# A's scores of a Nyström attention in 32x32 array tiles, transposed to tokens on VectorE

## The chip, the cores and the metric

One NeuronCore of a Trainium2 chip runs the whole kernel. The metric is the device time of one execution in microseconds. Before the change three runs took 265.65, 267.60 and 267.34 us (median 267.34). Engines are named by their profile letters where a view is quoted: PE is TensorE, PEld its weight loads, DVE is VectorE, ACT ScalarE, POOL GpSimd, SP SyncE.

## The reference

The inputs are q, k, v of 8 batches, 8 heads, 576 tokens and 64 dimensions, and two weight matrices of 512x2048 and 2048x512. Each batch goes through a Nyström attention with 32 landmarks, the means of 18 tokens each:

```
q_lm = q.reshape(B, H, 32, 18, D).mean(axis=3)
k_lm = k.reshape(B, H, 32, 18, D).mean(axis=3)
A  = softmax(scale * q @ k_lm^T)       # 576 x 32
Bm = softmax(scale * q_lm @ k_lm^T)    # 32 x 32
C  = softmax(scale * q_lm @ k^T)       # 32 x 576
Z  = Bm^T / (norm_1(Bm) * norm_inf(Bm) + 1e-6)
six times: Z = 2 Z - Z @ Bm @ Z
attention = A @ Z @ C @ v
```

The heads are put side by side as x (4608 tokens, 512 wide), and the result is `silu(x @ w_in) @ w_out`.

## The kernel before

**Stages.** The product Z C v of a batch is folded into w_in, which gives M (tile mb, 256 x 2048 per batch: 8 heads times 32 landmarks on two sets of 128 partitions). So the first layer is hps = M^T A^T, with A transposed (tile AT: landmark and head on the partition, tokens along the row). ScalarE's Silu turns hps into gT, and the second layer, ops, multiplies gT with w_out. ScalarE copies ops out and SyncE stores it.

**The order of work** is written out by hand. The loop at line 877 goes over the batches b; inside it 16 slots s. Each slot issues a piece of the first layer (`l1`, four matmuls), its Silu (`act`), and a counted number of second-layer matmuls (`l2_mm(cnt[s])`, from the lists CNT and REST), and between them lie the attention steps of the next batch, in the object `a` of class Att. With d = 0 from b = 2 on: slots 0 and 1 hold A's scores, B's and C's scores; slot 2 the exponentials (between two loads of ScalarE's function table, Exp and back to Silu); slots 3 to 9 the Newton steps of Z (`ns_mm` on TensorE, `ns_step` on VectorE), with the sums, reciprocals and products that normalise A in slots 4 to 7; slots 9 and 10 the last products of Z and C v (`x_out`, `z_mm`, `z_out`); slots 11 and 13 the M pairs (`m_pair`: mp and mpp). Slots 9, 10, 12 and 14 transpose q and k of the batch after the next on VectorE (`transpose_qk`, qkT), slots 4 and 8 form its landmarks on GpSimd, slot 13 transposes these (`lm_t`, lmc) and slot 15 starts its A scores, if that batch is 4 or later (`early`).

**A's scores before.** From batch 3 on (`sub`), tokens lie on the partition: for each chunk of 128 tokens and each half of the heads, qkT is the stationary operand and bd the moving one. bd is lmc spread block-diagonally over four heads, written by four GpSimd copies per batch (`bd_expand`). Five chunks go in three groups (`a_scores(0)`, `(1)`, `(2)`: 8, 8 and 4 matmuls) through the one-bank buffer "a". After each group VectorE takes the maximum over the 32 landmarks (`a_max`, nm) and subtracts it into xs in SBUF (`a_sub`). One ScalarE instruction takes all exponentials (`a_exp_all`, ex). VectorE sums them (`a_sum`), takes reciprocals (`a_rec`), GpSimd multiplies (`a_mul`, an), and for each chunk SyncE issues a DMA transpose of an into AT.

**Buffers around it.** The pool "h" has two buffers of two banks each. hps, scp (C's scores) and mpp take them in turn: a new user waits until the last reader of the buffer's earlier content is done. Engines execute their instructions in the order of issue.

Of the kernel before, what the change touches and what calls it, by code (L numbers as in the profile page):

```python
# [10 lines left out]
AF = mybir.ActivationFunctionType  # L11
OP = mybir.AluOpType
AX = mybir.AxisListType

# [24 lines left out]
def kernel(  # L41
# [9 lines left out]
    nc = tc.nc  # L51
# [28 lines left out]
    def ps2(nm):  # L80
        return psh.tile([128, 2, 512], FP, tag="h", name=nm)
# [159 lines left out]
    class Att:  # L241
# [300 lines left out]


        def a_first(self):
            self.nm = attp.tile([128, len(TCH), 8], BF, tag="nm", name="nm")
            if self.sub:
                self.xs = attp.tile([128, len(TCH), 256], FP, tag="xs", name="xs", bufs=1)

        def a_start(self):
            if not self.sub:  # L550
                self.a_first()
            self.ex = attp.tile([128, len(TCH), 256], BF, tag="ex", name="ex")
            self.arec = attp.tile([128, len(TCH), 8], FP, tag="arec", name="arec")
            self.an = attp.tile([128, len(TCH), 256], BF, tag="an", name="an")
            self.AT = AT_t[self.b] = attp.tile([128, 2, S], BF, tag="AT", name="AT")

        def a_dims(self, i):
            cc = list(range(2 * i, min(2 * i + 2, len(TCH))))
            return cc[0], len(cc), 128 if self.sub else TCH[cc[0]][1] - TCH[cc[0]][0]


        def a_scores(self, i):
            if i == 0 or self.sub:
                s = psa1("sa")
            elif self.b == 0:
                s = pso1("sa")
            else:
                s = pso1("sa") if i == 1 else self.bb[:, 128:384]
            self.sa[i] = s
            first = True  # L570
            for c in range(2 * i, min(2 * i + 2, len(TCH))):
                c0, c1 = TCH[c]
                if self.sub:
                    c0 = c1 - 128
                o = 256 * (c - 2 * i)
                ov = s[0:c1 - c0, o:o + 256].rearrange("p (r g n) -> p g r n", r=2, g=2)
                for g in range(2):
                    for e in range(2):
                        mm(ov[:, g].rearrange("p r (j l) -> p r j l", l=L),
                           self.qkT[:, 2 * g, c0:c1, e],  # L580
                           self.bd[:, g, :, e].rearrange("p (j r l) -> p r j l", r=2, l=L),
                           start=first, stop=(e == 1))
                        first = False

        def a_max(self, i, eng=nc.vector):
            c, n, pr = self.a_dims(i)
            with nc.allow_low_precision(reason="any shift common to a row's terms is exact"):
                eng.tensor_reduce(  # L588
                    out=self.nm[0:pr, c:c + n, :],
                    in_=self.sa[i][0:pr, 0:256 * n].rearrange("p (c h l) -> p c h l", h=8, l=L),  # L590
                    op=OP.max, axis=AX.X, negate=True)

# [4 lines left out]
                   .to_broadcast((pr, 8 * n, L)), start=False, stop=True)  # L597

        def a_sub(self, i):
            c, n, pr = self.a_dims(i)  # L600
            nc.vector.tensor_tensor(  # L601
                out=self.xs[:, c:c + n, :].rearrange("p c (h l) -> p (c h) l", l=L),
                in0=self.sa[i][:, 0:256 * n].rearrange("p (m l) -> p m l", l=L),
                in1=self.nm[:, c:c + n, :].rearrange("p c h -> p (c h)").unsqueeze(2)
                    .to_broadcast((128, 8 * n, L)), op=OP.add)


        def a_exp_all(self):
# [7 lines left out]
                                 scale=sc if self.mean else sc / SEG)  # L616

        def a_part(self, i):
            c, n, pr = self.a_dims(i)
            return (self.ex[0:pr, c:c + n, :].rearrange("p c (h l) -> p (c h) l", l=L),  # L620
                    self.arec[0:pr, c:c + n, :].rearrange("p c h -> p (c h)"))
# [13 lines left out]
                in1=r.unsqueeze(2).to_broadcast((128, 8, L)), op=OP.mult)  # L635

        def a_rec(self, i, n=1):
            c, _, pr = self.a_dims(i)
            r = self.arec[0:pr, c:min(c + 2 * n, len(TCH)), :].rearrange("p c h -> p (c h)")
            nc.vector.reciprocal(out=r, in_=r)  # L640
# [4 lines left out]
            self.a_mul(i)  # L645

        def a_mul(self, i):
            c, n, pr = self.a_dims(i)
            x, r = self.a_part(i)
            nc.gpsimd.tensor_tensor(  # L650
                out=self.an[0:pr, c:c + n, :].rearrange("p c (h l) -> p (c h) l", l=L), in0=x,
                in1=r.unsqueeze(2).to_broadcast((pr, 8 * n, L)), op=OP.mult)
            if self.by_dma:
                for m in range(c, c + n):
                    c0, c1 = TCH[m]
                    nc.sync.dma_start(out=self.AT[:, :, c0:c1],
                                      in_=self.an[pr - (c1 - c0):pr, m, :], transpose=True)


        def a_transpose(self, k, bank=None):  # L660
# [98 lines left out]
    def l2_mm(n):  # L759

        st = l2_state
        while n > 0 and st["queue"]:
# [18 lines left out]

    CNT = {0: [0, 0, 0, 0, 4, 4, 2, 2, 4, 4, 2, 2, 2, 2, 2, 2],
           1: [2, 2, 2, 2, 2, 6, 8, 8] + [4, 3] * 4,
           2: [5, 4, 12, 14, 3, 3, 3, 2, 4, 3, 3, 3, 4, 3, 3, 3]}
    REST = [5, 4, 12, 12, 3, 3, 2, 2, 4, 4, 4, 3, 4, 3, 4, 3]


# [89 lines left out]
    for b in range(B):  # L877
# [14 lines left out]
        for s in range(NDC):  # L892
# [46 lines left out]
            elif s == d + 1:  # L939
                l1(s)  # L940
                act(s)
                l2_mm(cnt[s])
                if a.sub and not a.early:
                    a.a_scores(1)
                    a.a_max(1)
                    a.a_sub(1)
                if b == 0:

                    transpose_qk(1, ORD[s])
                    a.lm_t(1)  # L950
                    a.bd_expand(0, 2, nc.gpsimd.tensor_copy)
                    for i in (1, 2):
                        a0.a_scores(i)
                        a0.a_max(i)
                a.b_scores()
                a.c_scores()
                if a.early:
                    a.a_scores(2)
                a.b_max()
                a.c_max(0)  # L960
                table(AF.Exp)
# [5 lines left out]
            elif s == d + 2 and a.sub:  # L967
                a.a_start()
                a.c_max(1)
                if not a.early:  # L970
                    l2_mm(4)
                    a.a_scores(2)
                a.a_max(2)
                a.a_sub(2)
                a.c_exp(0)
                a.c_exp(1)
                a.a_exp_all()
                a.b_norm()
                l2_mm(cnt[s] if a.early else cnt[s] - 4)
                table(AF.Silu)  # L980
                l1(s)
            elif s == d + 2:
# [82 lines left out]
            elif s == d + 3:  # L1065
                l1(s)
                act(s - 1)
                act(s)
                l2_mm(2)
                a.f_mm()  # L1070
                a.b_scale()
                a.f_out()


                nc.gpsimd.tensor_copy(out=gate, in_=a.fx[:, :, 0])  # L1075
                l2_mm(cnt[s] - 2)
                a.ns_mm()
            elif s <= d + 8:
                l1(s)
                if s == d + 6:  # L1080
                    a.w_mm()
                a.ns_step()
                act(s)
                if s == d + 4:
                    a.a_sum(0)
                elif s == d + 5:
                    a.a_sum(1)
                elif s == d + 6:
                    a.w_scale()
                    a.w_out()  # L1090
                    a.a_rec(0, 2)
                    a.a_mul(0)
                    a.a_mul(1)
                elif s == d + 7:
                    a.a_norm(2)
                l2_mm(cnt[s])
                a.ns_mm(last=(s == d + 8))
            elif s == d + 9:
                l1(s)
                a.x_out()  # L1100
                act(s)
                l2_mm(cnt[s])
            elif s == d + 10:
                l1(s)
                a.z_mm()
                a.z_out()
                act(s)
                l2_mm(cnt[s])
            else:
                l1(s)  # L1110
                act(s)
                if s in (d + 11, d + 13):
                    a.m_pair(s - d - 11)
                l2_mm(cnt[s])
# [8 lines left out]
            elif b + 2 < B:  # L1123
# [7 lines left out]
                if s == 13 and b > 1:  # L1131
                    ready = Att(b + 2)
                    ready.lm_t(0, 2)
                    ready.bd_expand(0, 2, nc.gpsimd.tensor_copy)
                ts = (9, 10, 12, 14) if d == 0 else (10, 11, 12, 13)
                if s in ts:
                    transpose_qk(b + 2, ORD[ts.index(s)])
                if s == 15 and b == 1:
                    ready = Att(b + 2)
                    ready.lm_t(0, 2)  # L1140
                    ready.bd_expand(0, 2, nc.gpsimd.tensor_copy)
                if s == 15 and ready.early:
                    ready.a_first()
                    ready.a_scores(0)
                    ready.a_max(0)
                    ready.a_sub(0)
            if (b, s) == (0, 3):
                l2_state["queue"] += [(0, 0)]
            elif s == 7:
# [32 lines left out]
```

## Time and profile before

| | |
|---|---|
| median of three runs | 267.34 us (265.65 to 267.60) |
| the profiled execution | 265.63 us, of it the span 263.9 us |
| granted TensorE clock over the span | 1.000 |
| second layer, ops | 576 matmuls, 146.1 us busy |
| first layer, hps | 512 matmuls, 82.8 us busy |
| A's scores, sa from bd and qkT | 152 matmuls, 12.3 us busy |
| Silu, gT from hps | 128 instructions, 82.7 us busy, 651 ns each |
| q/k transposes, qkT | 32 instructions, 38.7 us busy |
| GpSimd's normalising, an | 23 instructions, 20.1 us busy |
| DMA transposes of an into AT | 30 issues, 3.8 us median to landing |

The span runs from the first to the last instruction. The busy share says how long an engine had an instruction in flight. The chain of waits is followed back from the last instruction: at each step to what released it, or to the instruction in front of it on its engine; its pieces in order of time give the start, the time on the chain, the engine, and the tile written. Rows of the groups give line, engine, operation, output and inputs with their sizes, how often, the sum of busy us, the mean ns of one, and the idle time before them with its releaser. A timeline row gives start, duration, engine, line and operation. All matmuls share line 77, since a helper issues them, so they are told apart by their tiles.

### The profile page before, as it was taken

What the parts mean: (1) busy time and instruction counts of PE and PEld (TensorE: products, weight loads), DVE (VectorE), ACT (ScalarE), POOL (GpSimd) and SP (SyncE); (2) the same over time, 40 slices, a digit from 0 to 9 for tenths busy, and PEclk for the clock granted to TensorE, in tenths of its full rate; (3) what the DMA queues carried; (4) which work ended last, traced back from release to release, by engine and by line L of the source; (5) the groups of instructions that cost most, each with busy time, mean ns of one, the idle gap of its engine ahead of it and who ended that gap; (6) DMA issues with size and microseconds to landing.
All of it is one profiled execution on the core that took longest, in us unless ns stands there. A gap on an engine that the chain in (4) does not pass through costs nothing.

```text
span 263.9 us, 6736 instructions
## 1 busy us (share of the span) xinstructions
PE 254.5 (96%) x2755; PEld 143.4 (54%) x2755; DVE 161.1 (61%) x397; ACT 173.1 (66%) x314; POOL 118.3 (45%) x169
## 2 busy tenths in 40 slices
PE   8989989999999999999999999999999999999994
PEld 3647544475555456555655565555555564555541
DVE  5878874558597868876786778686778653000000
ACT  2377955769757785869575966687577947536511
POOL 7716424314698169744885189408950030100000
PEclk9999999999999999999999999999999999999999
DMA  7999999984983962878197927513471612121122
GB/s 222 202 211 206 203 206 219 186 151 75 197 151 78 197 150 41 147 142 182 50 134 164 200 73 98 117 32 112 54 164 40 103 60 67 40 80 42 40 80 80
DMA packets 37790, 32.93 MB, mean 125 GB/s; under 512 B 18816, under 2 KB 29056, under 8 KB 37760
## 3 DMA queue, kind: packets, MB, share of 16 engines
q0 software_dynamic: 14816, 17.76, 41.8%
q1 hardware_dynamic: 22944, 14.75, 22.0%
q8 instruction: 21, 0.34, 0.5%
q14 instruction: 9, 0.07, 0.1%
HBM read 36.70 MB, written 9.44 MB: 175 GB/s over the span
## 4 chain that ended last, share of the span: by engine, by line
PE 85%; DVE 7%; ACT 4%; DMA 2%; issue 1%; POOL 1%; ACTq 0%; POOLq 0%
PE ops L77 46%; PE hps L77 23%; PE lmp L77 3%; PE bb L77 3%; PE sa L77 3%; PE mp L77 2%; DVE cmx L445 2%; DMA raw<-in_k_dram 2%; PE scp L77 1%; PE wp L77 1%; PE mpp L77 1%; ACT eC L455 1%; ACT ex L614 1%; DVE nm L588 1%; PE atp L672 1%
## 5 line engine op out<-in xcount | busy, mean ns | idle before, releaser
L77 PE MATMUL ops<-w_out_sb,gT 128*128 128x512 bf16 x576 | 146.1, 379 | 0.0
L751 ACT ACTIVATE gT<-hps 128x576 bf16<-128x576 f32 (+2 forms) x128 | 82.7, 651 | 55.9 <-PE hps L77 55.2
L77 PE MATMUL hps<-AT,mb 128*128 128x288 bf16 (+2 forms) x512 | 82.8, 286 | 0.4 <-ACT AT L679 0.2
L77 PEld LDWEIGHTS <-gT 128*128 128x128 bf16 x576 | 53.0, 98 | 47.3 <-issue 5.9
L77 PEld LDWEIGHTS <-mb 128*128 128x128 bf16 x512 | 47.7, 98 | 24.9 <-issue 1.8
L200 DVE STREAM_TRANSPOSE qkT<-nat 128x576 f32<-128x576 f32 x32 | 38.7, 1239 | 0.3
L777 ACT COPY ost<-ops 128x512 f32<-128x512 f32 x36 | 21.0, 582 | 12.4 <-PE ops L77 12.3
L650 POOL TENSOR_TENSOR an<-ex,arec 128x512 bf16<-128x512 bf16 (+2 forms) x23 | 20.1, 897 | 18.0 <-DVE arec L640 16.0
L404 DVE SCALAR_TENSOR_TENSOR fx<-fx,bb 128x320 bf16<-128x320 bf16 (+1 forms) x39 | 16.6, 427 | 16.7 <-PE bb L77 16.2
L226 POOL TENSOR_TENSOR lma<-nat 128x1152 f32<-128x1152 bf16 x10 | 23.8, 2376 | 0.0
L717 DVE CAST mb<-mp 128x512 bf16<-128x512 f32 x28 | 18.0, 685 | 9.0 <-PE mp L77 8.9
L1075 POOL CAST gate<-fx 128x2 f32<-128x2 bf16 x6 | 1.1, 186 | 45.5 <-DVE fx L374 45.5
L162 ACT ACT_TABLE_LOAD x16 | 20.5, 1283 | 1.1 <-PEq L1166 0.8
L588 DVE TENSOR_REDUCE nm<-sa 128x16 bf16<-128x512 f32 (+2 forms) x22 | 13.2, 613 | 9.7 <-PE sa L77 9.7
L276 POOL COPY bd<-lmc 32x128 bf16<-32x128 bf16 x32 | 9.2, 286 | 15.0 <-DVE lmc L268 9.0
L77 PEld LDWEIGHTS <-fx 32*32 32x32 bf16 (+1 forms) x168 | 8.1, 93 | 12.6 <-DVE fx L404 3.5
L718 ACT CAST mb<-mpp 128x1024 bf16<-128x1024 f32 x14 | 14.2, 1011 | 0.6 <-PE mpp L77 0.6
L77 PE MATMUL bb<-fx 32*32 32x64 bf16 (+2 forms) x168 | 13.1, 205 | 0.7 <-DVE fx L404 0.3
L77 PEld LDWEIGHTS <-qkT 128*128 128x128 bf16 (+1 forms) x160 | 10.0, 98 | 6.4 <-DVE xs L601 2.7
L625 DVE TENSOR_REDUCE arec<-ex 128x16 f32<-128x512 bf16 (+2 forms) x23 | 13.4, 584 | 0.0
L77 PE MATMUL sa<-bd,qkT 128*128 128x128 bf16 (+1 forms) x152 | 12.3, 221 | 0.2 <-DVE xs L601 0.2
L445 DVE TENSOR_REDUCE cmx<-scp 128x1 f32<-128x576 f32 x16 | 11.9, 752 | 0.8 <-PE scp L77 0.5
(118 smaller groups left out, 259.2 us busy)
## 6 DMA issues: line engine op xcount, KB each, us to landing
out_dram<-ost SPq DMA_DIRECT2D x36, 256.0 KB, 2.2
v<-in_v_dram POOLq DMA_DIRECT2D x8, 576.0 KB, 7.1
nat<-in_k_dram POOLq DMA_DIRECT2D x15, 288.0 KB, 6.0
nat<-in_q_dram POOLq DMA_DIRECT2D x15, 288.0 KB, 7.0
w_in_sb<-in_moe_w_in_dram POOLq DMA_DIRECT2D x4, 512.0 KB, 14.5
w_out_sb<-in_moe_w_out_dram POOLq DMA_DIRECT2D x4, 512.0 KB, 13.5
raw<-in_k_dram SPq DMA_DIRECT2D x1, 576.0 KB, 4.1
raw<-in_q_dram SPq DMA_DIRECT2D x1, 576.0 KB, 5.0
```

The source lines that it names most:

```text
L77: nc.tensor.matmul(out=o, lhsT=lhsT, rhs=rhs, start=start, stop=stop, skip_group_check=True)
L162: nc.scalar.activation(out=spare[:, 1:2], in_=spare[:, 0:1], func=func)
L200: nc.vector.transpose(out=o.rearrange("p (l t) -> p t l", t=SEG), in_=nat_t[b][:, j, :].bitcast(FP).rearrange("p (t l) -> p t l", l=L))
L226: nc.gpsimd.tensor_tensor(out=a1, in0=nat[:, :, 0:3 * w], in1=nat[:, :, 3 * w:6 * w], op=OP.add)
L404: nc.vector.scalar_tensor_tensor(out=n, in0=self.fx, scalar=2.0, in1=self.p, op0=OP.mult, op1=OP.add if self.tiled else OP.subtract)
L445: nc.vector.tensor_reduce(out=mx, in_=self.s[g][:, :, 0:HF], op=OP.max, axis=AX.XY, negate=True)
L588: eng.tensor_reduce(out=self.nm[0:pr, c:c + n, :], in_=self.sa[i][0:pr, 0:256 * n].rearrange("p (c h l) -> p c h l", h=8, l=L), op=OP.max, ...
L650: nc.gpsimd.tensor_tensor(out=self.an[0:pr, c:c + n, :].rearrange("p c (h l) -> p (c h) l", l=L), in0=x, in1=r.unsqueeze(2).to_broadcast(( ...
L717: nc.vector.tensor_copy(out=o[:, r, 0:512], in_=m[r])
L718: nc.scalar.copy(out=o[:, :, 512:1024], in_=m2)
L751: nc.scalar.activation(out=gT_t[b][:, 2 * s:2 * s + 2, o + c0:o + c1], in_=h[:, :, 0:c1 - c0], func=AF.Silu)
L777: nc.scalar.copy(out=ost, in_=st["ps"])
```

## The change

From batch 3 on the landmarks of k become the stationary operand (32x32 slices of lmc) and q's transposed tokens the moving one, in array tiles of 32x32. Scores come in two groups of 288 tokens, 16 matmuls each, landmark on the partition, in a buffer of the pool "h". VectorE transposes them in blocks of 32x32 from PSUM into xs, which puts the token on the partition, and takes the maximum there; GpSimd subtracts it in place. Exponentials, sums, reciprocals and products work on the new layout, two parts for three. The five DMA transposes become two block transposes on VectorE (`a_back`), in slots 9 and 14. `bd_expand` goes for these batches. The q/k transposes of loops 2 to 5 move from slots 9, 10, 12, 14 to 7, 8, 10, 12. Batch 3's second scores move in front of part of the second-layer matmuls of slot 1, and the list CNT for b = 2 is rewritten with the same sum of 72.

```diff
+                self.nm = attp.tile([128, 2, 2, SEG // 2], FP, tag="nmt", name="nm")
...
+        def a_view(self, x):
+            return (x.rearrange("p c n -> p (c n)")[:, 0:2 * S]
+                    .rearrange("p (f r t l) -> p f r t l", f=2, r=2, l=L))
...
         def a_scores(self, i):
-            if i == 0 or self.sub:
+            if self.sub:
+                s = self.sa[i] = ps2("sa")
+                for e in range(2):
+                    for g in range(2):
+                        for h in range(4):
+                            p, j = slice(32 * h, 32 * h + 32), 2 * g + h // 2
+                            mm(s[32 * j:32 * j + 32, h % 2, 0:HF], self.lmc[p, 2 * g + 1, :, e],
+                               self.qkT[p, 2 * g, HF * i:HF * i + HF, e],
+                               start=(e == 0), stop=(e == 1))
+                return
...
         def a_max(self, i, eng=nc.vector):
+            if self.sub:
+                nc.vector.transpose(
+                    out=self.xs[:, i],
+                    in_=self.sa[i][:, :, 0:HF].rearrange("p r (t n) -> p r t n", n=L))
+                eng.tensor_reduce(out=self.nm[:, i], in_=self.xs[:, i], op=OP.max, axis=AX.X,
+                                  negate=True)
+                return
...
         def a_sub(self, i):
-            c, n, pr = self.a_dims(i)
-            nc.vector.tensor_tensor(
-                out=self.xs[:, c:c + n, :].rearrange("p c (h l) -> p (c h) l", l=L),
-                in0=self.sa[i][:, 0:256 * n].rearrange("p (m l) -> p m l", l=L),
-                in1=self.nm[:, c:c + n, :].rearrange("p c h -> p (c h)").unsqueeze(2)
-                    .to_broadcast((128, 8 * n, L)), op=OP.add)
+            nc.gpsimd.tensor_tensor(
+                out=self.xs[:, i], in0=self.xs[:, i],
+                in1=self.nm[:, i].unsqueeze(3).to_broadcast((128, 2, SEG // 2, L)), op=OP.add)
...
         def a_mul(self, i):
+            x, r = self.a_part(i)
+            if self.sub:
+                nc.gpsimd.tensor_tensor(
+                    out=self.an[:, i].rearrange("p r t l -> p (r t) l"), in0=x,
+                    in1=r.unsqueeze(2).to_broadcast((128, SEG, L)), op=OP.mult)
+                return
...
+        def a_back(self, i):
+            nc.vector.transpose(
+                out=self.AT[:, :, HF * i:HF * i + HF].rearrange("p r (t n) -> p r t n", n=L),
+                in_=self.an[:, i])
...
-           2: [5, 4, 12, 14, 3, 3, 3, 2, 4, 3, 3, 3, 4, 3, 3, 3]}
+           2: [5, 8, 12, 12, 3, 3, 2, 2, 4, 3, 3, 3, 3, 3, 3, 3]}
...
             elif s == d + 1:
                 l1(s)
                 act(s)
-                l2_mm(cnt[s])
                 if a.sub and not a.early:
+                    l2_mm(3)
                     a.a_scores(1)
                     a.a_max(1)
                     a.a_sub(1)
+                    l2_mm(cnt[s] - 3)
+                else:
+                    l2_mm(cnt[s])
...
-                if a.early:
-                    a.a_scores(2)
...
             elif s == d + 2 and a.sub:
                 a.a_start()
                 a.c_max(1)
-                if not a.early:
-                    l2_mm(4)
-                    a.a_scores(2)
-                a.a_max(2)
-                a.a_sub(2)
                 a.c_exp(0)
                 a.c_exp(1)
                 a.a_exp_all()
                 a.b_norm()
-                l2_mm(cnt[s] if a.early else cnt[s] - 4)
+                l2_mm(cnt[s])
...
-                elif s == d + 7:
+                elif s == d + 7 and not a.sub:
                     a.a_norm(2)
...
-                    ready.bd_expand(0, 2, nc.gpsimd.tensor_copy)
-                ts = (9, 10, 12, 14) if d == 0 else (10, 11, 12, 13)
+                ts = (7, 8, 10, 12) if d == 0 else (10, 11, 12, 13)
...
+            if nxt and b > 1 and s in (9, 14):
+                a.a_back((9, 14).index(s))
```

More of the change, by code (lines that the diff above doesn't have):

```diff
@@ L544, in a_first @@
         def a_first(self):
-            self.nm = attp.tile([128, len(TCH), 8], BF, tag="nm", name="nm")
             if self.sub:
-                self.xs = attp.tile([128, len(TCH), 256], FP, tag="xs", name="xs", bufs=1)
+                self.nm = attp.tile([128, 2, 2, SEG // 2], FP, tag="nmt", name="nm")
+                self.xs = self.a_view(attp.tile([128, len(TCH), 256], FP, tag="xs", name="xs",
+                                                bufs=1))
+            else:
+                self.nm = attp.tile([128, len(TCH), 8], BF, tag="nm", name="nm")
+        def a_view(self, x):
+            return (x.rearrange("p c n -> p (c n)")[:, 0:2 * S]
+                    .rearrange("p (f r t l) -> p f r t l", f=2, r=2, l=L))
         def a_start(self):
@@ L554, in a_start @@
             self.an = attp.tile([128, len(TCH), 256], BF, tag="an", name="an")
+            if self.sub:
+                self.ex, self.an = self.a_view(self.ex), self.a_view(self.an)
             self.AT = AT_t[self.b] = attp.tile([128, 2, S], BF, tag="AT", name="AT")
@@ L558, in a_dims @@
             cc = list(range(2 * i, min(2 * i + 2, len(TCH))))
-            return cc[0], len(cc), 128 if self.sub else TCH[cc[0]][1] - TCH[cc[0]][0]
+            return cc[0], len(cc), TCH[cc[0]][1] - TCH[cc[0]][0]
         def a_scores(self, i):
-            if i == 0 or self.sub:
+            if self.sub:
[8 more added lines that the diff above has]
+                return
+            if i == 0:
                 s = psa1("sa")
@@ L572, in a_scores @@
                 c0, c1 = TCH[c]
-                if self.sub:
-                    c0 = c1 - 128
                 o = 256 * (c - 2 * i)
@@ L618, in a_part @@
         def a_part(self, i):
+            if self.sub:
+                m = SEG
+                r = self.arec.rearrange("p c h -> p (c h)")[:, m * i:m * i + m]
+                return self.ex[:, i].rearrange("p r t l -> p (r t) l"), r
             c, n, pr = self.a_dims(i)
@@ L637, in a_rec @@
         def a_rec(self, i, n=1):
+            if self.sub:
+                r = self.arec.rearrange("p c h -> p (c h)")[:, 0:2 * SEG]
+                nc.vector.reciprocal(out=r, in_=r)
+                return
             c, _, pr = self.a_dims(i)
@@ L647, in a_mul @@
         def a_mul(self, i):
+            x, r = self.a_part(i)
+            if self.sub:
+                nc.gpsimd.tensor_tensor(
+                    out=self.an[:, i].rearrange("p r t l -> p (r t) l"), in0=x,
+                    in1=r.unsqueeze(2).to_broadcast((128, SEG, L)), op=OP.mult)
+                return
             c, n, pr = self.a_dims(i)
-            x, r = self.a_part(i)
             nc.gpsimd.tensor_tensor(
@@ L946 @@
                     a.a_sub(1)
+                    l2_mm(cnt[s] - 3)
+                else:
+                    l2_mm(cnt[s])
                 if b == 0:
@@ L1140 @@
                     ready.lm_t(0, 2)
-                    ready.bd_expand(0, 2, nc.gpsimd.tensor_copy)
                 if s == 15 and ready.early:
```

## The prediction

> **What bounds the kernel now.** I read the page first: busy shares, then the chain of waits.
>
> ```profile
> PE 254.5 (96%) x2755; PEld 143.4 (54%) x2755; DVE 161.1 (61%) x397; ACT 173.1 (66%) x314; POOL 118.3 (45%) x169
> ...
> PE 85%; DVE 7%; ACT 4%; DMA 2%; issue 1%; POOL 1%; ACTq 0%; POOLq 0%
> ```
>
> TensorE is both the busiest engine and the chain. So I next read the chain in order of time through the head of one batch (the loop over batch 4, whose attention is batch 5's; the heads at 112, 169 and 197 us repeat it, 28.3 us apart), and the chain at the M pairs some us before.
>
> ```profile
> 133.76 0.34 PE mp L77 x8
> 134.10 0.22 PE mpp L77 x8
> 134.32 0.75 PE ops L77 x3
> ...
> 140.72 0.46 PE sa L77 x8
> ...
> 142.75 0.58 PE sa L77 x8
> 143.33 0.49 PE hps L77 x4
> 143.82 0.86 PE ops L77 x4
> ...
> 144.88 0.52 PE scp L77 x28
> 145.41 0.34 PE sa L77 x4
> 145.74 2.59 PE ops L77 x12
> ...
> 152.16 0.49 PE hps L77 x4
> ```
>
> Columns are start, us on the chain, and what. No engine but TensorE appears (hps is the first product of the second computation, ops its second), so here TensorE's own work sets the time, and A's scores are 0.46 + 0.58 + 0.34 = 1.38 us of it per batch. Whether others stay hidden is read from ScalarE's and VectorE's timelines over the same head.
>
> ```profile
> 144.53 1.28 ACT L162 ACT_TABLE_LOAD   x1
> ...
> 147.34 0.74 ACT L455 ACTIVATE eC<-scp,cbs 128x576 bf16<-128x576 f32 x1
> ...
> 148.14 1.27 ACT L609 ACTIVATE ex<-xs 128x1280 bf16<-128x1280 f32 x1
> ...
> 151.30 1.17 ACT L751 ACTIVATE gT<-hps 128x576 bf16<-128x576 f32 x2
> ```
>
> ScalarE runs without a gap from slot 1's Silu to slot 2's (150 to 152 us). Slot 2's ends about 151.30 + 0.58 = 151.89 and frees the buffer that the hps at 152.16 needs: 0.27 us to spare. VectorE is the engine that feeds this chain: its second cbs ends at 147.25, just before the exp at 147.34.
>
> **TensorE's part.** Removed per batch: 20 matmuls, 1.38 us. Added: two excursions of 16 matmuls, 32x32, 288 columns, eight distinct tiles per half of the contraction. The nearest row is the M pair: 16 small-tile matmuls of 512 columns cost 0.34 + 0.22 us and 0.10 of the ops after it (0.75 against 0.65 for three), so 0.22 per eight and about 0.22 for entering and leaving. With 288 columns: 2 x 0.22 x 288/512 + 0.22 = 0.47 us. Two make 0.94. Leaving scp, now paid inside the third sa, falls on the ops: 0.10. New total 1.04, a saving of 0.34 us per batch. The 32 matmuls of scp (same tile size and columns, two rows to a column and two columns to a row, as here) take about 0.55 us, which is the same rate of eight at a time.
>
> [...]
>
> **VectorE's part at the head.** Removed: three maxima and three subtractions (0.69, 0.69, 0.69, 0.69, 0.41, 0.42 us: 3.6). Added: two block transposes of 576 fp32 from PSUM and two maxima of 576 from SBUF. A maximum: 0.69 for 512, 0.75 for cmx's 576; I take 0.75. The block transpose T is not in the trace, and these are the nearest rows.
>
> ```profile
> L200 DVE STREAM_TRANSPOSE qkT<-nat 128x576 f32<-128x576 f32 x32 | 38.7, 1239 | 0.3
> L445 DVE TENSOR_REDUCE cmx<-scp 128x1 f32<-128x576 f32 x16 | 11.9, 752 | 0.8 <-PE scp L77 0.5
> L268 DVE STREAM_TRANSPOSE lmc<-lmn 128x128 f32<-128x128 f32 x7 | 2.1, 305 | 4.6 <-ACT lmn L217 3.9 <-POOL lmn L234 0.6
> ```
>
> L200 has T's size at 1.24, but writes with a step of 18 elements; L268 writes in one run as T does, and with its other size in the same view (64 elements, two times, 212 ns: slope 1.45 ns) extends to 0.305 + 448 x 0.00145 = 0.95. One pass over 576 fp32 of PSUM is 0.75 (cmx). I take 0.95, nearest in writing, and keep 0.75 and 1.24.
>
> [...]
>
> Walk through the head with T = 0.95. First excursion 140.72 to 141.19; T0 141.27 to 142.22, maximum to 142.97. hps and five ops bring TensorE to 142.76; the second excursion needs the buffer T0 freed at 142.22 (0.5 spare; the scores now draw on the two two-bank buffers that hps and scp use, so slot 0's hps also waits for slot 15's Silu, done at 140.76, and not slot 14's). T1 143.30 to 144.25, maximum to 145.00. hps ends at 143.72, ops at 144.58, bb at 144.75, where scp needs T1's buffer: 0.5 spare. b_max starts at 145.00 (144.96 before), and the second cbs ends 2.29 later as before: 147.29. ScalarE could begin that exp 3.52 after hps' end as before, at 147.24: a delay of 0.1, given back by A's exponentials (1152 columns for 1280, about 0.11 by the slope from 576 at 0.65). Slot 2's Silu ends 8.06 after hps' end, and the hps that needs it comes at 8.34 - 0.34 + 0.10 = 8.10. No stall, 0.04 spare. Every 0.1 us of T beyond 0.95 is 0.1 of stall: at 1.24, 0.25, and the 0.34 shrinks to 0.09; at 0.75 nothing more is won.
>
> **GpSimd and SyncE.** GpSimd loses four bd copies (1.27) and 0.3 of the normalising (1152 columns, 2.63 for 1280), and gains two subtractions. fp32 with 384 takes 1.00, with 128 0.46: 1.4 for 576; bf16 512 with a broadcast 1.05, so 1.2 to 1.4. The second starts at 145.00 and ends by 146.4, and A's exponentials want it at 148.2. Behind each, which waits for VectorE's maximum, are queued the tail copy in odd batches (read only when slots 8 and later work on that batch) and the four q/k load issues for the batch three ahead (4 x 0.55, moved from 140.3 to about 147; landing 7 us later, first read in the next batch's slot 4). Neither is on the chain. SyncE loses five AT transposes per batch, in whose queue the out stores stand; no wait on a store shows in the chain, so nothing is won.
>
> **VectorE later.** The q/k transposes move to slots 7, 8, 10, 12. After slot 7's Newton step (156.60 to 157.03) one of 1.25 runs to 158.25, so slot 8's step (before at 157.51) ends at 158.66; its matmul stands at 158.77: 0.1 spare, cover that was 0.8. The next transpose ends 159.9, x_out 160.35, z_mm at 160.66: 0.3 spare. a_back(0) is a 16-bit block transpose of 576 (bounds as T; L328's 64 take 0.245): to 161.3, behind it z_out to 161.6, with mp at 162.08: 0.45. It waits for GpSimd's first normalising (about 158). Slot 13's casts and lm_t end near 167.2, a_back(1) 168.2, the next T0 about 169.6. The sums grow from 0.68 to 0.75 and have 0.19 idle behind them; the third sum, reciprocal and GpSimd part go. I charge 0.2 us over all batches for these thin covers; nothing else.
>
> **Batch 3's head** (loop over batch 2) is different: the chain there runs over VectorE.
>
> ```profile
> 85.47 0.70 DVE nm L588
> ...
> 89.37 0.67 DVE cmx L445
> ...
> 91.15 0.84 ACT eC L455 x2
> ...
> 92.03 0.65 PE hps L77 x4
> ```
>
> From 84.97 to the Newton matmul at 95.82 are 10.85 us with 30 ops matmuls. The new sequence has 32 and, without a stall, 0.47 + 0.49 + 0.65 + 0.47 + 1.08 + 0.17 + 0.57 + 0.10 + 2.59 + 0.98 + 0.43 + 0.11 + 2.16 = 10.27; the two more ops are 0.43 taken from later, so 9.84: 1.0 won. With T = 0.95, 0.1 stall at the second excursion and 0.2 at the hps after slot 2's Silu: 0.7 won. With 1.24 about 0.3, with 0.75 1.0.
>
> **Sum.** 4 x 0.34 + 0.7 - 0.2 = 1.9 us. The profiled execution is 265.63 us (span 263.9 and 1.7 around it) and becomes 263.7; it stands 1.7 under the median of the three, 267.34, which becomes 265.4. With T at 1.24: 4 x 0.09 + 0.3 = 0.7 won; at 0.75: 1.4 + 1.0 = 2.4. So 264.9 to 266.7 on the median.
>
> **Rivals.**
> Slower: VectorE takes over the batch's head, if a transpose out of PSUM costs more than L200 (for it: L200's 2.15 ns per element, and no instruction here transposes out of PSUM; against: L268, cmx). It decides from T = 1.3, where 0.34 is eaten. At 1.9, the second excursion waits 0.5 for T0, scp 0.66 for T1, the hps after slot 2's Silu 0.55: 1.7 against 0.34, 1.4 lost per batch; in batch 3's head about 1.1. Together 6.7: 274.0.
>
> [...]
>
> More is won: excursions of small tiles hide most of entry and exit (0.18 of 0.22 each), as scp does behind bb, and all covers hold: 4 x (0.34 + 2 x 0.18) + 1.0 = 3.8, 263.5. Against: the M pair pays its entry each time.
>
> **How the numbers follow.** A per cent is 2.7 us, about what a measurement here can tell from no change; the three runs differ by 0.7%. Chances: forecast 0.60, slower rival 0.18, half rate 0.07, more won 0.15. Faster by over 1%: 0.15 and 0.06 from the forecast's upper end with the scatter, 0.21; slower 0.18 and 0.02, 0.20; within, 0.59. The range leaves out the slow rival's 0.18: from 263.2 (more won) to 268.4 (half rate with the scatter); likeliest 264.9 to 266.7.
>
> **What would show it.** Right: in the chain sa twice per head near 0.47, ops after scp 0.10 longer, and no VectorE between; VectorE's new row at 0.8 to 1.0; ScalarE gapless up to slot 2's Silu; hps there without idle. Wrong: the T row above 1.3; TensorE idle before the second sa, scp or that hps; 16 sa matmuls at 0.7 (half rate); idle before the Newton matmul of slot 8.

## The result, and the profile after

Four runs of the changed kernel took 276.43 to 282.43 us, median 276.86; four of the kernel before had 265.59 to 267.60, median 266.50. The ratio is 1.038 (95% interval 1.034 to 1.042): slower, by some 10 us, where the forecast was 265.4 from 267.34, a change too small to tell from none. The profiled execution took 276.43 us, its span is 274.6. Ratios leave out slow runs (282.43 here), and medians under 3 us apart are read beside the periods of the loops, since some executions, among them the profiled ones of the first three experiments, show a mean granted clock of 0.992 to 0.993, where that of the kernel before shows 1.000, and start the first scores of loop 2 at 86.4 to 86.9 us for 84.8.

The page of the kernel after, its busy shares, the chain of waits by engine and the head of the chain by line:

```profile
PE 251.2 (91%) x2772; PEld 139.5 (51%) x2815; DVE 167.6 (61%) x387; ACT 172.9 (63%) x314; POOL 122.3 (45%) x154
...
PE 68%; DMA 11%; DVE 8%; ACT 7%; issue 3%; POOL 1%; ACTq 0%; POOLq 0%
PE ops L80 35%; PE hps L80 20%; DMA eCT<-eC 10%; PE lmp L80 3%; DVE cmx L448 3%; PE mp L80 2%; PE bb L80 2%; PE sa L80 2%; DMA raw<-in_k_dram 2%; ACT L165 1%; ACT ex L634 1%; ACT eC L458 1%; PE wp L80 1%; PE mpp L80 1%; DVE bbs L304 1%
```

TensorE had 96% and 85% in these rows and has 91% and 68%. DMA went from 2% of the chain to 11%, nearly all of it one transfer that no step of the prediction mentions: eCT<-eC, the DMA transposes of C's exponentials, which the products wp in slot 6 read. The last line has another name new there: VectorE's bbs.

The chain of the kernel after, in order of time, through the head of the loop over batch 4 (start, us on the chain, what):

```profile
149.43 0.38 PE sa L80 x16
149.80 0.59 PE hps L80 x4
...
151.48 0.38 PE sa L80 x15
151.85 0.60 PE hps L80 x4
...
153.52 0.52 PE scp L80 x27
...
157.18 0.19 ACT eC L458
157.38 0.58 ACT ex L634
157.96 7.10 DMA eCT<-eC
```

The two excursions of TensorE are there as costed: 0.38 us each for 16 matmuls, and 0.59 for the hps behind instead of 0.49, so 0.48 together (0.47 in the prediction). But this chain does not go on over TensorE: it leaves through ScalarE and runs into 7.10 us of a DMA transpose.

Where the 10.7 us of span went, from the first score matmul of one loop to that of the next (called the period of the loop below):

| loop over batch | before, us | after, us | difference |
|---|---|---|---|
| start to loop 2 | 84.81 | 84.95 | +0.14 |
| 2 | 27.43 | 29.14 | +1.71 |
| 3 | 28.31 | 35.27 | +6.96 |
| 4 | 28.32 | 29.38 | +1.06 |
| 5 | 28.31 | 28.62 | +0.31 |
| 6 to the end | 66.72 | 67.24 | +0.52 |

Loops 2 to 4 issue q/k loads (for batches 5 to 7); loops 5 and 6 have none left. The large losses stand where loads are, and a smaller one is everywhere.

**Loop 3, where most is lost.** GpSimd's timeline of the kernel after (start, duration, engine, line, operation):

```profile
116.26 1.16 POOL L628 TENSOR_TENSOR xs<-xs,nm 128x576 f32<-128x576 f32 x1 [4.96 <-DVE nm L611]
118.31 1.16 POOL L628 TENSOR_TENSOR xs<-xs,nm 128x576 f32<-128x576 f32 x1 [0.90 <-DVE nm L611]
119.41 1.04 POOL L799 COPY gT<-gT 128x1024 bf16<-128x1024 bf16 x1
120.39 0.58 POOL L108 DMA_DIRECT2D nat<-in_k_dram  x1
...
122.01 0.56 POOL L108 DMA_DIRECT2D nat<-in_q_dram  x1
```

SyncE's queue and TensorE, two timelines of the same loop:

```profile
121.28 2.85 SPq L465 DMA_TRANSPOSE eCT<-eC  x2
```

```profile
128.29 0.65 PE L80 MATMUL hps<-AT,mb 128*128 128x288 bf16 x4
133.21 1.14 PE L80 MATMUL wp<-v,eCT 96*32 96x64 bf16 x48 [4.27 <-DMA eCT<-eC]
```

The four loads queue on GpSimd behind both subtractions (and here the tail copy) and are issued from 120.39 on; the two transposes follow at 121.28. In the kernel before, GpSimd's first load and SyncE's transposes of this loop were:

```profile
113.56 0.58 POOL L105 DMA_DIRECT2D nat<-in_k_dram  x1
```

```profile
119.03 2.60 SPq L462 DMA_TRANSPOSE eCT<-eC  x2
```

There 5.5 us lay between the first load and the transposes, and now 0.9. The tile view of eCT, of the kernel before and of the one after:

```profile
DMA to landing us min/median/max: 2.8/3.8/8.2
```

```profile
DMA to landing us min/median/max: 2.8/7.5/11.9
```

TensorE stands 4.27 us in front of wp in this loop.

The stall has an echo. Windows of 3 us of the kernel after (busy us and count of PE, PEld, DVE, ACT, POOL, then the granted clock, the DMA share and GB/s):

```profile
130.00:133.00 3.00, 0.00 (x0) 0.00 (x0) 0.00 (x0) 0.00 (x0) 0.00 (x0) 0.67 1.29 96
133.00:136.00 3.00, 2.34 (x54) 1.69 (x56) 1.08 (x3) 0.00 (x0) 0.75 (x1) 0.50 0.53 189
136.00:139.00 3.00, 3.00 (x15) 1.62 (x14) 2.58 (x4) 1.31 (x3) 2.99 (x4) 0.69 0.00 0
```

All five engines are idle in the first, and in the next two TensorE is granted 0.50 and 0.69 of its clock: the 48 wp matmuls take 1.14 us for 0.56 before. In windows of 0.5 us the clock is 0.50 to 0.51 from 131.0 to 137.5 and 1.00 again from 138.0. From 133.2 on TensorE works in that stretch, some 4.6 us, and an estimated 2.3 of them are lost; with the wait of 4.27 and the 0.31 that loop 5 loses too, this makes 6.9 of the loop's 6.96.

**The loss in every loop.** VectorE's and GpSimd's timelines of the kernel after:

```profile
153.59 0.23 DVE L298 TENSOR_REDUCE bmx<-bb 128x2 f32<-128x64 f32 x1
153.85 0.91 DVE L304 TENSOR_SCALAR bbs<-bmx 128x2 f32<-128x2 f32 x1
154.67 0.74 DVE L448 TENSOR_REDUCE cmx<-scp 128x1 f32<-128x576 f32 x1
...
157.84 0.17 DVE L367 TENSOR_SCALAR n<-n 128x2 f32<-128x2 f32 x1
```

```profile
153.58 1.16 POOL L628 TENSOR_TENSOR xs<-xs,nm 128x576 f32<-128x576 f32 x1 [0.89 <-DVE nm L611]
```

bbs scales two numbers per partition. The tile view of bbs in the kernel before has:

```profile
L301 DVE TENSOR_SCALAR bbs<-bmx x5: 168/169/171, 89.2 to 201.8; 128x2 f32<-128x2 f32 x5
```

Before it took 168 to 171 ns, now 907 to 1093: it starts while GpSimd's second subtraction runs and ends where that ends (153.85 + 0.91 = 154.76; 153.58 + 1.16 = 154.74). An operation of the same kind and size with no subtraction beside it, at 157.84, takes 0.17. In the loop over batch 5, free of loads, the chain shows what that does:

```profile
183.23 0.91 DVE bbs L304
184.14 0.67 DVE cmx L448
...
189.80 0.55 ACT gT L795
190.35 0.04 issue
190.39 0.65 PE hps L80 x4
```

From the end of the B scores (bb) the chain goes over their maximum, bbs, the two maxima of C, the exponentials, the table load and the Silu to the hps that was forecast to have 0.04 us to spare.

So two theories, both about what GpSimd's subtraction brings with it and not about TensorE. **Loads:** the q/k loads, issued late behind the subtractions, run at the same time as the eCT transposes and delay them. **Lock:** VectorE's bbs waits until GpSimd's subtraction is done. The rival to both is the prediction's own: VectorE's new work, the transposes and maxima, is simply too long for the head.

### The profile page after: what moved, and what is told of

Its sections match the earlier page's. It is cut to its first block, busy times and chain, and to the rows that moved or that the text cites. A ratio compares the mean times of both kernels' runs of the same rounds, so it can differ in the third digit from the quotient of the medians.

```text
span 274.6 us, 6722 instructions
## 1 busy us (share of the span) xinstructions
PE 251.2 (91%) x2772; PEld 139.5 (51%) x2815; DVE 167.6 (61%) x387; ACT 172.9 (63%) x314; POOL 122.3 (45%) x154
## 4 chain that ended last, share of the span: by engine, by line
PE 68%; DMA 11%; DVE 8%; ACT 7%; issue 3%; POOL 1%; ACTq 0%; POOLq 0%
PE ops L80 35%; PE hps L80 20%; DMA eCT<-eC 10%; PE lmp L80 3%; DVE cmx L448 3%; PE mp L80 2%; PE bb L80 2%; PE sa L80 2%; DMA raw<-in_k_dram 2%; ACT L165 1%; ACT ex L634 1%; ACT eC L458 1%; PE wp L80 1%; PE mpp L80 1%; DVE bbs L304 1%
## 5 line engine op out<-in xcount | busy, mean ns | idle before, releaser
L80 PE MATMUL ops<-w_out_sb,gT 128*128 128x512 bf16 x537 | 139.8, 381 | 4.0 <-issue 3.0
L80 PE MATMUL hps<-AT,mb 128*128 128x288 bf16 (+2 forms) x512 | 84.3, 288 | 1.9 <-ACT eC L458 1.0
L203 DVE STREAM_TRANSPOSE qkT<-nat 128x576 f32<-128x576 f32 x32 | 38.7, 1240 | 0.2
L628 POOL TENSOR_TENSOR xs<-xs,nm 128x576 f32<-128x576 f32 x10 | 11.6, 1158 | 32.4 <-DVE nm L611 32.4
L683 POOL TENSOR_TENSOR an<-ex,arec 128x576 bf16<-128x576 bf16 x10 | 11.4, 1158 | 17.2 <-DVE arec L669 17.2
L608 DVE STREAM_TRANSPOSE xs<-sa 128x576 f32<-128x576 f32 x10 | 7.8, 783 | 9.5 <-PE sa L80 9.4
L654 DVE TENSOR_REDUCE arec<-ex 128x18 f32<-128x576 bf16 (+2 forms) x18 | 12.1, 671 | 0.0
L80 PE MATMUL wp<-v,eCT 96*32 96x64 bf16 x384 | 5.2, 201 | 6.8 <-DMA eCT<-eC 6.4
L688 POOL TENSOR_TENSOR an<-ex,arec 128x512 bf16<-128x512 bf16 (+1 forms) x8 | 7.0, 882 | 9.6 <-DVE arec L673 7.6
L799 POOL COPY gT<-gT 128x1024 bf16<-128x1024 bf16 x4 | 4.1, 1037 | 15.8 <-ACT gT L795 15.8
```

The costliest lines, as they stand in the source:

```text
L80: nc.tensor.matmul(out=o, lhsT=lhsT, rhs=rhs, start=start, stop=stop, skip_group_check=True)
L203: nc.vector.transpose(out=o.rearrange("p (l t) -> p t l", t=SEG), in_=nat_t[b][:, j, :].bitcast(FP).rearrange("p (t l) -> p t l", l=L))
L628: nc.gpsimd.tensor_tensor(out=self.xs[:, i], in0=self.xs[:, i], in1=self.nm[:, i].unsqueeze(3).to_broadcast((128, 2, SEG // 2, L)), op=OP.add)
L654: nc.vector.tensor_reduce(out=r, in_=x, op=OP.add, axis=AX.X)
```

## The experiments

**The loads alone, and the scaling alone.** The first kernel issues the loads in slot 15 of the loop before, ahead of the first subtraction; the second moves bbs to ScalarE, the third does both.

```diff
 after, loads early
-                if s == (5 if b == 1 else 1) and b + 3 < B:
+                if b == 1 and s == 5:
                     load_qk(b + 3)
+                if s == 15 and b + 4 < B:
+                    load_qk(b + 4)
 after, bbs on ScalarE
-            nc.vector.tensor_scalar(out=self.bbs, in0=bmx, scalar1=s2, scalar2=None, op0=OP.mult)
+            nc.scalar.mul(out=self.bbs, in_=bmx, mul=s2)
```

> The changed kernel, with the four q/k loads issued in slot 15 ahead of the first subtraction in GpSimd's queue, no longer behind the second one. Theory L (the loads, held in GpSimd's queue behind the subtractions, run at the same time as the DMA transposes of eCT, which come late for the products that read them): the waits of TensorE on eCT (6.4 us at the matmuls and 7.8 at the weight loads) vanish, the median falls by 7 to 9 us to 268 to 270. Rival V (VectorE's later chain at the batch's head is what costs, the eCT waits follow from it): at most 2 us fall, 275 or more, and eCT stays late.

Loads early: median 268.17 us of 10 runs against 266.37 before, ratio 1.006 (1.004 to 1.009). By the ratios that is 8.5 us of the 10.2 back. The tile view of eCT in this kernel:

```profile
DMA to landing us min/median/max: 2.7/2.8/8.4
```

TensorE no longer waits for these transposes. The periods are 27.33, 28.62, 28.62, 28.63: the loss tied to loads is gone, and the one of 0.31 per loop that the kernel after had in loop 5 now stands in each of loops 3 to 5. bbs still takes 905 to 1094 ns.

> The changed kernel, with the scaling of B's maximum (bbs, 128x2, 0.91 to 1.09 us in the changed kernel and 0.17 before) moved from VectorE to ScalarE. Theory P (VectorE's bbs waits for GpSimd's subtraction, which is running at that moment): about 0.75 us leave VectorE's chain in each of five batches; in the batches without loads (0.3 to 0.5 us slower than before) the time falls to 0.3 below that of before, so 3 us in all if the eCT waits do not eat it, 273 to 275. If only the loads matter (theory L alone): 276 to 277.

bbs on ScalarE: 274.06 us of 4 runs, ratio 1.030 (1.026 to 1.034), by the ratios 2.2 us less than the kernel after, with waits on eCT still there. The time is in the range expected from the lock, but not for its reason: the periods of loops 2 to 5 are 29.50, 30.58, 29.42 and 28.80, so only loop 3 is shorter, where TensorE waits 1.21 and 0.35 us for eCT and not 4.27; the others are 0.04 to 0.36 longer.

> Both edits together: loads early and bbs on ScalarE. If L and P are the whole of the loss, what is left is the forecast for the change without them: 0.34 us less per batch and 0.7 to 1.0 in batch 3's head, 264.1 to 265.5 with the median of before at 266.5, ratio 0.990 to 0.997. If more is missing, 266 or more.

Both: 269.41 us of 6 runs, ratio 1.010 (1.007 to 1.013). This missed: it was to be faster than the early loads alone, and its median is 1.2 us above them (the intervals overlap; the periods of loops 3 to 5, 28.80 for 28.62, give 0.5 of it). ScalarE's timeline says why:

```profile
145.68 0.65 ACT L795 ACTIVATE gT<-hps 128x576 bf16<-128x576 f32 x1 [0.56 <-PE hps L80]
...
147.04 0.20 ACT L304 ACTIVATE bbs<-bmx 128x2 f32<-128x2 f32 x1 [0.71 <-DVE bmx L298]
147.26 1.28 ACT L165 ACT_TABLE_LOAD   x1
```

On ScalarE bbs stands in front of the Exp table load, and waits 0.71 us there for bmx. The load, which could have run in that gap, starts when bbs is through, and the chain goes over ScalarE. So this edit takes a wait away and puts in another; what bbs on ScalarE won without the early loads says nothing of the lock. It needed an edit that leaves bbs where it is.

**The old layout with late loads.** If the loads are the cause, the kernel before must lose too when its loads are held until bbs, with nothing else of the change in it.

```diff
 before
                 if s == (5 if b == 1 else 1) and b + 3 < B:
+                    if b > 1:
+                        nc.gpsimd.tensor_copy(out=gate, in_=a.bbs)
                     load_qk(b + 3)
```

> The kernel before, with one GpSimd copy of bbs ahead of the q/k loads of three batches, so that they are issued some 4.5 to 5 us later, about where the changed kernel issues them; nothing else is touched. Theory L: the products that read eCT wait here too, most in the loop over batch 3; 271 to 275. If the changed layout or VectorE is the cause and not the loads: 266 to 267, as before.

273.36 us of 4 runs (270.18 to 275.72), ratio 1.022 (1.016 to 1.027). In loop 2 the loads are issued from 90.45 us and the transposes at 91.64, 1.2 apart. The tile view of eCT in this kernel:

```profile
DMA to landing us min/median/max: 2.8/7.8/9.2
```

TensorE waits for eCT in front of wp in each of loops 2 to 4 (1.38 and 0.33 us in loop 2), and in none of the kernel before. TensorE's timeline in loop 2:

```profile
100.88 0.36 PE L77 MATMUL wp<-v,eCT 96*32 96x64 bf16 x24 [1.38 <-DMA eCT<-eC]
```

The old layout loses by the same wait.

**The subtraction back on VectorE.**

```diff
 after
         def a_sub(self, i):
-            nc.gpsimd.tensor_tensor(
+            nc.vector.tensor_tensor(
```

> The changed kernel with only the subtraction put back on VectorE (in place in xs, 576 fp32, about 0.75 each); GpSimd has nothing in front of the loads, and nothing to collide with. Theories L and P: eCT waits gone, bbs at 0.17, but two subtractions of 0.75 now in VectorE's chain, of which about 1.05 us reach it (0.3 ahead of the second transpose, 0.75 behind its maximum) for the 0.74 that bbs lost: the batch 28.7 to 29.0, median 267.5 to 270. If another part of the change (the transposes, the array tiles) were the cause: 273 or more.

268.26 us of 10 runs against 266.53, ratio 1.007 (1.004 to 1.011). With the subtractions gone from GpSimd, both symptoms go: eCT lands in 2.8 us (median), and the tile view of bbs has:

```profile
L304 DVE TENSOR_SCALAR bbs<-bmx x5: 168/168/169, 90.2 to 204.2; 128x2 f32<-128x2 f32 x5
```

What is left is the prediction's rival with its own cause: the chain of the head then reads sa, T0 0.79, maximum 0.76, subtraction 0.76, T1 0.70, maximum 0.76, subtraction 0.76, B's maximum, bbs and cmx on VectorE, and the periods of loops 3 to 5 are 28.71.

**Early loads, and bbs split.** bbs as two instructions of 128x1 stays on VectorE, beside the subtraction, in the same place of the queue.

```diff
 after, loads early
-            nc.vector.tensor_scalar(out=self.bbs, in0=bmx, scalar1=s2, scalar2=None, op0=OP.mult)
+            for g in range(2):
+                nc.vector.tensor_scalar(out=self.bbs[:, g:g + 1], in0=bmx[:, g:g + 1], scalar1=s2,
+                                        scalar2=None, op0=OP.mult)
```

> Loads early as in the first run, and bbs kept on VectorE, but as two instructions of 128x1 in place of one of 128x2. Theory P2 (what waits for GpSimd's subtraction is this form of instruction, the 128x2 scaling in SBUF, and not VectorE as a whole: the 128x2 maximum in front of it reads PSUM and ran at its usual 0.23): each of the two takes about 0.15, VectorE's chain is 0.6 us shorter per batch than with one, the batch falls from 28.62 us (loads early) to about 28.0, below the 28.31 of before; median 264.5 to 266, ratio 0.993 to 0.999. Rival W (VectorE cannot touch SBUF at all while that subtraction runs, or bbs waits for something else): the first of the two takes 0.7 to 0.9, the batch stays at 28.5 or more, 268.

265.22 us of 12 runs against 266.53, ratio 0.996 (0.993 to 0.999); periods 26.66, 28.25, 28.30, 28.24. VectorE's and GpSimd's timelines of this kernel:

```profile
144.37 0.22 DVE L305 TENSOR_SCALAR bbs<-bmx 128x1 f32<-128x1 f32 x2
144.60 0.76 DVE L450 TENSOR_REDUCE cmx<-scp 128x1 f32<-128x576 f32 x1
```

```profile
144.10 1.16 POOL L630 TENSOR_TENSOR xs<-xs,nm 128x576 f32<-128x576 f32 x1 [0.90 <-DVE nm L613]
```

Both halves run inside the subtraction's time and take 144 to 154 ns each, 0.22 together. Against the early loads alone 2.9 us are won by the medians, and 2.4 from the first scores of loop 2 to the end in the profiled executions. That an instruction of half the size goes through, where the whole one is held to the subtraction's end, shows that the form of bbs decides, not the load on VectorE. The chain through the head is TensorE's again:

```profile
139.94 0.38 PE sa L80 x16
...
144.55 2.70 PE ops L80 x12
...
151.07 0.53 PE hps L80 x4
```

From the first sa to slot 4's hps are 11.13 us, before 11.44: 0.31 won, where the prediction has 0.34. But the periods of loops 3 to 5 are only 0.02 to 0.07 shorter, in this loop 0.02, so it is given back later, between that hps and the first M pair: 10.21 us for 9.92. There, in slots 6 and 7, this is VectorE's timeline:

```profile
154.69 0.35 DVE L494 TENSOR_TENSOR wsp<-wsc,parity 128x4 f32<-128x4 f32 x1
155.15 0.42 DVE L513 TENSOR_TENSOR wz<-wp,wsp 128x256 bf16<-128x256 f32 x1
155.53 0.38 DVE L671 RECIPROCAL arec<-arec 128x36 f32<-128x36 f32 x1
155.83 0.43 DVE L409 SCALAR_TENSOR_TENSOR fx<-fx,bb 128x320 bf16<-128x320 bf16 x1
```

wsp took 0.16 before and 0.35 here, beside GpSimd's lmn (154.57, 0.46); the reciprocal has 36 columns for 32. The Newton step fx behind them comes late: from 153.71 the chain runs over VectorE and these rows, to TensorE's bb that needs fx.

```profile
156.31 0.31 PE bb L80 x2
```

**Which part of the later slots.** The same kernel with the q/k transposes back in their old slots 9, 10, 12 and 14:

> The kernel with loads early and bbs in two, with the q/k transposes put back in slots 9, 10, 12 and 14. If their move matters (the two transposes towards tokens in slots 9 and 14 then stand in VectorE's queue beside them), the batch grows by 0.2 us or more over that kernel's; my covers of 0.1 to 0.45 us say that either place holds and the batch is the same within 0.1, with the first scores of the next batch the place where it would show (slot 14's two transposes end about 1 us before them).

One execution took 265.13 us, with periods of 26.67, 28.24, 28.29 and 28.24: no change to speak of. The moved transposes, which the prediction charged with thin covers, are not where the 0.29 goes. Then w_scale (the wsc reciprocals and wsp) from slot 6 to slot 3, ahead of the landmark's GpSimd work, in that kernel and in the one before:

```diff
 after, loads early, bbs split      (and, alone, before)
                 l2_mm(2)
                 a.f_mm()
                 a.b_scale()
+                if a.sub:
+                    a.w_scale()
                 a.f_out()
...
                 elif s == d + 6:
-                    a.w_scale()
+                    if not a.sub:
+                        a.w_scale()
                     a.w_out()
```

> The kernel with loads early and bbs in two, with the four small VectorE instructions that scale W (wsc three times, wsp; 0.65 us) moved from slot 6 to slot 3, ahead of the first Newton operand, where VectorE then idles 1.87 us. Theory C (the head of the batch wins the 0.31 us that was forecast and the Newton slots give 0.29 back: slot 7's step waits for VectorE, which spends 0.35 on wsp while GpSimd's lmn runs and 0.38 on the longer reciprocal, with 0.15 us of cover before the change): slot 7's products come without a wait, the batch falls from 28.25 to 27.9 to 28.05, median 263.7 to 265.0, ratio 0.989 to 0.995. Rival (the time is lost elsewhere in these slots, in the moved q/k transposes for instance): 28.2 or more, 265.

264.24 us of 6 runs against 266.09, ratio 0.992 (0.989 to 0.994). It is the fastest kernel of this study, 1.0 us under the one without the move by the medians; its periods of loops 2 to 5 (26.47 and three times 28.04) are 0.86 shorter together. wsp on VectorE's timeline and slot 7's bb on the chain, in the same loop:

```profile
148.68 0.16 DVE L494 TENSOR_TENSOR wsp<-wsc,parity 128x4 f32<-128x4 f32 x1
```

```profile
155.91 0.14 PE bb L80 x2
```

wsp has its 0.16 again, and TensorE is alone on the chain through loop 4.

> The kernel before with the same move alone. Theory C: slot 7 was covered there, so nothing is won: the batch 28.3, median 265.5 to 267.3, ratio 0.997 to 1.003. If the move is a gain by itself, 265 or less, and what the other kernel wins by it is not the change's.

The kernel before gains nothing from it: 266.07 us of 10 runs against 266.09, ratio 1.000 (0.998 to 1.002). Its slot 7 was not late.

## Why the prediction was wrong

The forecast of 265.4 us and the range of 263.2 to 268.4 missed 276.86. One step failed for most of it, a second for the rest.

- **The step that failed: "Neither is on the chain."** The prediction saw that the q/k loads move on GpSimd's queue from 140.3 to about 147 us and asked only when they must land (in time: no wait on them is in the chain). It didn't ask what else the DMA engines do from 147 on. The eCT transposes, issued from another queue just then (in the trace of before at 147.34), land late, and TensorE waits for them. Early loads alone bring some 8.5 us back (ratio 1.038 to 1.006), and late loads alone cost the old layout 5.8 (0.022 of 266.4; 4.5 in the spans of the profiled executions).
- **The second: "the second cbs ends 2.29 later as before".** The length of that row was carried over though the change puts a subtraction on GpSimd beside it. From the start of bmx to the end of the second cbs it was 153.59 to 156.46, 2.87 us. With bbs split it is 144.11 to 146.40: 2.29 exactly. With 0.04 us to spare in front of the hps that needs slot 2's Silu, more than half of the excess of 0.58 shows: 0.67 us in loop 2 and 0.32 to 0.39 in loops 3 to 5 (periods with early loads, bbs whole and split). Worth 2.4 to 2.9 us.
- **A term too small: 0.2 us for the thin covers.** It was 0.9 to 1.0 once the two costs were gone (periods, medians), and in slot 7, not in the step of slot 8 that the prediction watched. It is no part of the 276.86: wsp took its 161 ns there and ran into lmn only when the head was quicker. The cover in slot 7 was not looked at, since only the instructions added and moved were, not those (wsp) that run beside GpSimd at other times than before.
- **TensorE's part was right.** An excursion is 0.48 us for 0.47, the ops after scp are 0.11 longer for 0.10 (2.70 against 2.59 for twelve), the saving in the head 0.31 for 0.34. Batch 3's loop won 0.77 (27.43 to 26.66) for 0.7.
- **The prices of the new instructions were near.** Groups of the kernel after:

```profile
L608 DVE STREAM_TRANSPOSE xs<-sa 128x576 f32<-128x576 f32 x10 | 7.8, 783 | 9.5 <-PE sa L80 9.4
L628 POOL TENSOR_TENSOR xs<-xs,nm 128x576 f32<-128x576 f32 x10 | 11.6, 1158 | 32.4 <-DVE nm L611 32.4
```

T is 0.78, within its bounds of 0.75 to 1.24 but well under the 0.95 taken: the lower bound, one pass like cmx, was the better one. The subtraction is 1.16, just under 1.2 to 1.4. What these instructions do to their neighbours had no price.
- **The rivals.** "Slower" had the sign and nearly the size (274.0), which was luck: its condition was a T above 1.3, and T was 0.78. Its mechanism, VectorE's head on the chain, appeared for another reason: bbs, or, with the subtraction on VectorE, two more instructions there. Half rate, from which the upper end of the range, 268.4, and a chance of 0.07 come, is shown by no run: 16 matmuls take 0.38, where the prediction gave 0.7 as its sign. "More is won" fell with the excursions' full price.

Without the two costs the change does about what was forecast: a ratio of 0.996 (0.993 to 0.999) for the kernel with early loads and split bbs, or 1.1 us won of 266.5; with w_scale moved too 0.992 (0.989 to 0.994), 2.2 us. The profiled spans are 0.8 and 1.5 shorter than before's. The forecast was 1.9.

Not tried: loads issued after the transposes, or fewer at a time. What inside the DMA engines holds a transpose up beside loads is not visible in these traces; shown is that moving the loads in time, and nothing else, makes the wait come and go in both layouts. Why TensorE waits 4.27 us for them in loop 3, 1.59 in loop 2 and 0.54 in loop 4, with the loads and transposes close together in all three, is open.

## What to carry to other kernels

An instruction added to an engine's queue delays what stands behind it: here the loads of loop 3 moved from 1.3 to 6.3 us after its first scores, behind two subtractions that waited 4.96 and 0.90 us for nm. For a DMA issue the question is not only whether it still lands in time, but which other transfers are in flight at its new time, and who waits for those. A row's length from the old profile need not hold when other work runs on the other engines: on VectorE, beside GpSimd, bbs went from 0.17 to 0.91 us and wsp from 0.16 to 0.35. So list what each row of a thin path will run beside, before its number is carried over. A path with 0.04 us to spare should be priced as if it were on the chain.

## What the runs showed of the hardware

- Engines take their instructions in the order of issue where these timelines bear on it: bbs on ScalarE waits 0.71 us for bmx and runs from 147.04 for 0.20, and the table load behind it starts at 147.26; GpSimd's loads of loop 3 start at 120.39, when both subtractions and the tail copy are through.
- A VectorE operation of two elements per partition can be held until a GpSimd instruction ends: bbs, 128x2 from SBUF to SBUF, took 0.91 us beside a subtraction of 1.16 and 0.17 in the kernel before; in the form 128x1 it took 0.15 beside that subtraction. In the kernel with early loads and bbs split, wsp, 128x4 with two SBUF inputs, took 348 ns (median), for 162 before; a transpose out of PSUM beside the first subtraction keeps its 0.78 us. That one element per partition isn't held is read from these runs alone, and the hold itself is not in the trace; it is inferred from the times.
- Two DMA transposes that land in 2.8 us (median) with the loads issued early took up to 11.9 behind four loads of 288 KB whose issue began 0.9 to 1.9 us ahead of them. In the old layout the median was 3.8 us, with 5.5 us between loads and transposes in loop 3, and 7.8 with the loads held, 1.2 us ahead in loop 2. The loads are issued by GpSimd and the transposes by SyncE.
- TensorE's granted clock fell to 0.50 in the course of one wait, 2.1 us into its 4.27 us, and stayed there for some 6.8 us, so this wait cost more than its length. In loop 2 of the same kernel a wait of 1.26 us on the same transposes left it at 1.00; behind the longest wait with bbs on ScalarE, 1.66 us, 24 wp matmuls took 0.36 us, as they do behind the 1.26. That the wait is the cause is an inference from one case.
- A 32x32 block transpose of 576 fp32 elements per partition takes 783 ns from PSUM when written in one run, and 1240 from SBUF when written with a step of 18 elements (qkT).
